# Both ends of a tile loop reordered, logits made in two halves: retention attention with a soft mixture of experts on one core

## The chip, the core and the metric

The kernel runs on one core of one Trainium2 chip. Its time is device microseconds of one execution. The kernel before took 230.43 us, the median of three runs (228.4 to 231.46).

## The reference

```
scores = q @ k.T / 8                      # q, k, v: 8 batches, 8 heads, 576 positions, 64 wide
x = ((scores * decay[head]) @ v)          # decay = gamma ** (i - j) for i >= j, else 0; no softmax
x = x as 4608 rows of 512                 # heads side by side
logits = x @ phi                          # 512 x 32: 8 experts of 4 slots
d = softmax of logits over the 4608 rows
slot_input = d.T @ x                      # 32 rows of 512
slot_out[e] = relu(slot_input[e] @ w1[e]) @ w2[e]     # 512 -> 1024 -> 512, for each expert
c = softmax of logits over the 32 slots
out = c @ slot_out                        # 4608 x 512
```

All of it is float32. Two steps look at every row before anything can follow: the softmax over rows and the sum that makes the slots' inputs.

## The kernel before, in words

The rows are worked off as 36 tiles of 128 rows. For each pair of batches there are nine tiles: four chunks of 128 positions for each of the two batches in turn (`z` is 0 or 1), and one tile with the last 64 positions of both (`z` is 2). A tile's input (k, transposed q and v, 512 columns each, 768 KB together) is loaded into one of four slots of the tile `qb`.

A tile `i` of the loop goes through these steps, in this order on TensorE (PE):

- `scores(i)` multiplies transposed k (`kts`) with q (L165); VectorE (DVE) multiplies the result with the mask `mt` into `sts`, in two halves (L169).
- `inter(i)` adds what earlier chunks contribute, from the running state `sbs` (L184; not in the first chunk of a batch).
- `k_transpose(i + 1)` turns the next tile's k (L156), and ScalarE (ACT) copies it to `kts` (L157); `scale(i + 1)` lets GpSimd (POOL) multiply v by a decay (L144, needs table `vt`) and, where a chunk begins, makes the table `xt` from `gt` and `cf` (L146, L149).
- a share of the softmax work of four tiles that are already done (below).
- `values(i)` multiplies `sts` with v (L192); DVE multiplies the result with `xt` and writes the tile's x, transposed, into a ring of eight (`rg`, L195).
- `state(i)` updates the running state (L204) and ACT copies it (L206).

Group g is tiles 4g to 4g+3. Its softmax work is spread over tiles 4g+4 to 4g+7: in the first, `comb_3` of the group before and the logits (L226) with the running maximum and, behind `state`, the exponential; in the second and third, the transposes of the four x (L212), of the exponentials (L253) and of the logits (L271); in the fourth `slot_sums` (L260), which adds the group to the running sum `acc` with a rescaling factor.

Each engine executes its instructions in the order of the program, as written; a wait holds up all that is behind it on that engine. Loads of tiles and of expert weights (64 units of 512 KB) are all issued by SyncE (SP); the tables are issued by ACT at the start. 38 units go to tiles of their own (`ws`): four at the start, then one per tile. Seven more go where the loop's own buffers come free (`qb`, `sts`). The last 19 units wait until an earlier unit has been used: `release` issues the next load into that unit's tile, or, once all 64 are issued, keeps the tile for outputs.

After the loop the last group is worked off, then `lrun` and `acc` give the slots' inputs (L380, L394, L397), and the experts' first products begin with four units (L437, the first release), then the second products (L458) and the outputs (L478 to L484), 18 stores of 512 KB.

Of the kernel before, what the change touches and what calls it, by code (L numbers as in the profile page):

```python
# [8 lines left out]
F32 = mybir.dt.float32  # L9
# [28 lines left out]
def retention_softmoe(ctx, tc, qkv, wts, phi, mtab, vtab, gtab, ctab, msel, out):  # L38
    nc = tc.nc
# [12 lines left out]
    ps_x, ps_st, ps_t = psum("ps_x", 2), psum("ps_st", 1), psum("ps_t", 3)  # L52
# [4 lines left out]
    qb = const("qb", NQ * 1536)  # L57
    ws = [const(f"ws{i}", 1024) for i in range(NW)]
# [21 lines left out]
    unit_tile = []  # L80

    def load_w(t):
        if len(unit_tile) < 64:
            nc.sync.dma_start(out=t, in_=wts[len(unit_tile)])
            unit_tile.append(t)
            return True
        return False

    def load_t(t, parts=((0, 1536),)):
        for lo, hi in parts:  # L90
            nc.sync.dma_start(out=qb[:, t % NQ * 1536 + lo:t % NQ * 1536 + hi], in_=qkv[t][:, lo:hi])

    load_t(0, ((0, 512), (512, 1024), (1024, 1536)))
    for x, y in ((vt, vtab), (mt, mtab), (cf, ctab), (gt, gtab)):
        nc.scalar.dma_start(out=x, in_=y)
    load_t(1)
    load_w(ws[0])
    load_t(2)
    load_w(ws[1])
    load_t(3)  # L100
    load_w(ws[2])
    load_w(ws[3])
    late = [(phs, phi), (ms, msel)]

    wz = ets
# [47 lines left out]
    def k_transpose(t):  # L153
        pt = ps_t.tile([P, 512], F32, name="pt")
        for a in range(NP):
            nc.tensor.transpose(pt[:, a * P:(a + 1) * P], part(t, 0)[:, a * P:(a + 1) * P], ident)  # L156
        nc.scalar.copy(out=kts, in_=pt)  # L157
# [17 lines left out]
    def inter(t):  # L175
        p, c, z = order[t]
        if c == 0:
            return
        x = X_of(t)
        for y in ((z,) if z < 2 else (0, 1)):  # L180
            cols = slice(0, P) if z < 2 else R[y]
            for a in range(NP):
                for j in range(2):
                    nc.tensor.matmul(x[R[a % 2], j, a // 2, cols], lhsT=sb[R[j], y, a, :], rhs=qT(t)[R[j], a, cols],  # L184
                                     start=(a < 2 and y == (0 if z == 2 else z)), stop=True, skip_group_check=True)
# [19 lines left out]
                                 start=(c == 0 and z == 0 and a == 0), stop=True, skip_group_check=True)  # L205
        nc.scalar.copy(out=sb[:, z], in_=pst[:, z])  # L206

    def x_transpose(t, pt=None, eng=None):
        if pt is None:
            pt = ps_t.tile([P, 512], F32, name="pt")  # L210
        for a in range(NP):
            nc.tensor.transpose(pt[:, a * P:(a + 1) * P], xT[t][:, a * P:(a + 1) * P], ident)  # L212
        if eng is nc.vector:
            nc.vector.tensor_copy(out=xT[t], in_=pt)  # L214
        else:
            nc.scalar.copy(out=xT[t], in_=pt)  # L216
# [3 lines left out]

    galpha = {}

    def logit_products(pl, g, tiles):
        for a in range(NP):
            for i in tiles:
                nc.tensor.matmul(pl[i * NS:(i + 1) * NS, :], lhsT=phs[:, a, :], rhs=xT[4 * g + i][:, a * P:(a + 1) * P],  # L226
                                 start=(a == 0), stop=(a == NP - 1), skip_group_check=True)

    def logits(g):
        pl = ps_t.tile([P, 512], F32, name="pt")[:, 0:P]  # L230
        logit_products(pl, g, range(4))
        nc.scalar.copy(out=lt[:, g, :], in_=pl)
        no, nn = nrun[(g + 1) % 2], nrun[g % 2]
        if g == 0:
            nc.vector.tensor_reduce(out=nn, in_=lt[:, g, :], axis=AX.X, op=ALU.max, negate=True)
        else:
            ng = sm("ng")
            nc.vector.tensor_reduce(out=ng, in_=lt[:, g, :], axis=AX.X, op=ALU.max, negate=True)
            nc.vector.tensor_tensor(out=nn, in0=ng, in1=no, op=ALU.min)
# [11 lines left out]
    def e_transpose(g):  # L251
        pe = ps_t.tile([P, 512], F32, name="pt")[:, 0:P]
        nc.tensor.transpose(pe, ets, ident)  # L253
        nc.scalar.copy(out=ens, in_=pe)

    def slot_sums(g, pp=None):
        if pp is None:
            pp = ps_t.tile([P, 512], F32, name="pt")
        for i in range(4):
            nc.tensor.matmul(pp[i * NS:(i + 1) * NS, :], lhsT=ens[:, i * NS:(i + 1) * NS], rhs=xT[4 * g + i],  # L260
                             start=True, stop=True, skip_group_check=True)
        if g == 0:
# [6 lines left out]
    def comb_1(g):  # L269
        pn = ps_t.tile([P, 512], F32, name="pt")[:, 0:P]  # L270
        nc.tensor.transpose(pn, lt[:, g, :], ident)  # L271
        ln = pn.rearrange("p (i s) -> p i s", i=4)
        cmx = sm("cmx", 4)
        nc.vector.tensor_reduce(out=cmx, in_=ln, axis=AX.X, op=ALU.max)
        cc = cn.rearrange("p (i s) -> p i s", i=4)
        nc.vector.tensor_tensor(out=cc, in0=ln, in1=cmx.unsqueeze(2).broadcast_to([P, 4, NS]), op=ALU.subtract)
        nc.scalar.activation(out=cn, in_=cn, func=AF.Exp, scale=1.0)
# [10 lines left out]
    def comb_3(g):  # L288
        pc = ps_t.tile([P, 512], F32, name="pt")[:, 0:P]
        nc.tensor.transpose(pc, cn, ident)  # L290
        nc.scalar.copy(out=lt[:, g, :], in_=pc)

    k_transpose(0)
    scale(0)
    for i in range(NT):
        g, r = divmod(i - 4, 4)
        scores(i)
        inter(i)
        if i + 1 < NT:
            k_transpose(i + 1)  # L300
            scale(i + 1)
        if g >= 0:
            if r == 0:
                if g:
                    comb_3(g - 1)
                logits(g)
            elif r == 1:
                x_transpose(4 * g)
                x_transpose(4 * g + 1)
                e_transpose(g)  # L310
            elif r == 2:
                x_transpose(4 * g + 2)
                x_transpose(4 * g + 3)
                comb_1(g)
            else:
                slot_sums(g)
        if i == NT - 1:
            pl = ps_st.tile([P, 512], F32, name="pst")[:, 0:P]
            logit_products(pl, NG - 1, range(3))
        values(i)  # L320
        state(i)
        if g >= 0:
            if r == 0:
                expo(g)
            if r == 2:
                comb_2(g)
        if i + NQ < NT:
            load_t(i + NQ)
        if late and i > 0:
            x, y = late.pop(0)  # L330
            nc.sync.dma_start(out=x, in_=y)
        if len(unit_tile) < NW:
            load_w(ws[len(unit_tile)])
    while len(unit_tile) < NW:
        load_w(ws[len(unit_tile)])
    for u in range(6):
        load_w(qb[:, u * 1024:(u + 1) * 1024])
    load_w(sts)

# [6 lines left out]
    g = NG - 1  # L346
    no, nn = nrun[(g + 1) % 2], nrun[g % 2]
    delta, far = ms[:, 0:P], ms[:, P:P + NS]
    x_transpose(4 * g)
    x_transpose(4 * g + 1, eng=nc.vector)  # L350
    logit_products(pl, g, range(3, 4))
    ng = sm("ng")
    nc.vector.tensor_reduce(out=ng, in_=pl, axis=AX.X, op=ALU.max, negate=True)
    nc.vector.tensor_tensor(out=nn, in0=ng, in1=no, op=ALU.min)
    rs = sm("rs")
    nc.scalar.activation(out=ets, in_=pl, func=AF.Exp, bias=nn, scale=1.0, accum_out=rs)
    x_transpose(4 * g + 2, eng=nc.vector)
    x_transpose(4 * g + 3, eng=nc.vector)
    pm = ps_x.tile([P, 2, 512], F32, name="sx")[:, 0, 0:P]
    nc.tensor.transpose(pm, nn.broadcast_to([P, P]), ident)  # L360
    e_transpose(g)
    alpha = sm("alpha")
# [10 lines left out]
    dl = sm("dl", NS)  # L373
    nc.vector.tensor_scalar(out=dl, in0=delta[:, 0:NS], scalar1=fa, scalar2=None, op0=ALU.mult)
    nc.vector.scalar_tensor_tensor(out=lrun, in0=lrun, scalar=alpha, in1=rs, op0=ALU.mult, op1=ALU.add)
    slot_sums(g)
    nc.scalar.copy(out=lt[:, g, :], in_=pl)
    comb_3(g - 1)
    pd = ps_t.tile([P, 512], F32, name="pt")
    nc.tensor.matmul(pd[:, 0:NS], lhsT=lrun.broadcast_to([P, P]), rhs=dl, start=True, stop=True)  # L380
    rv = sm("rv", NS)
# [197 lines left out]
```

## Time and profile before

| | |
|---|---|
| the profiled execution | 231.0 us |
| its span, first to last instruction | 229.2 us |
| PE busy, with 3994 matmuls and 3994 weight loads | 208.5 us (91%) |
| DVE, ACT, POOL busy | 115.0, 77.0, 61.2 us |
| moved by DMA | 72.59 MB, mean 317 GB/s |
| mean granted TensorE clock | 0.967 of full |

Busy shares are averages over three different stages: the start, the loop of tiles (to about 161 us) and the experts. A bracket at the end of a timeline's row holds the idle time of that engine just before it and what ended it; "issue" means that nothing which the profile shows was waited for. PE's times are modelled at their ends, so matmuls overlap slightly in the rows.

### The profile page before, as it was taken

What the parts mean: (1) busy time and instruction counts of PE and PEld (TensorE: products, weight loads), DVE (VectorE), ACT (ScalarE), POOL (GpSimd) and SP (SyncE); (2) the same over time, 40 slices, a digit from 0 to 9 for tenths busy, and PEclk for the clock granted to TensorE, in tenths of its full rate; (3) what the DMA queues carried; (4) which work ended last, traced back from release to release, by engine and by line L of the source; (5) the groups of instructions that cost most, each with busy time, mean ns of one, the idle gap of its engine ahead of it and who ended that gap; (6) DMA issues with size and microseconds to landing.
All of it is one profiled execution on the core that took longest, in us unless ns stands there. A gap on an engine that the chain in (4) does not pass through costs nothing.

```text
span 229.2 us, 8978 instructions
## 1 busy us (share of the span) xinstructions
PE 208.5 (91%) x3994; PEld 158.2 (69%) x3994; DVE 115.0 (50%) x234; ACT 77.0 (34%) x191; POOL 61.2 (27%) x65
## 2 busy tenths in 40 slices
PE   8498969999989999999999999999979999999910
PEld 7387859788779788789788789789752235555600
DVE  1245425847644866864764855755672201045820
ACT  2121244154235235255245154155130101136710
POOL 1461454242351335244144315341310000000000
PEclk9889999999999999999999999999997999999975
DMA  7999996789896789988778979898640999989996
GB/s 206 387 417 406 409 357 239 251 302 345 322 343 237 274 274 349 321 324 306 280 283 323 329 261 375 298 370 295 206 182 16 378 416 412 407 342 377 396 405 246
DMA packets 18181, 72.59 MB, mean 317 GB/s; under 512 B 2272, under 2 KB 2528, under 8 KB 18144
## 3 DMA queue, kind: packets, MB, share of 16 engines
q1 hardware_dynamic: 17568, 71.47, 84.1%
q8 instruction: 31, 0.51, 0.9%
q10 hardware_dynamic: 576, 0.56, 0.7%
q14 instruction: 6, 0.05, 0.1%
HBM read 62.58 MB, written 9.44 MB: 314 GB/s over the span
## 4 chain that ended last, share of the span: by engine, by line
PE 83%; DMA 7%; DVE 3%; issue 2%; SPq 1%; ACT 0%; DVEq 0%
PE sx L192 16%; PE sx L165 11%; PE pt L156 8%; DMA qb<-in_qkv 7%; PE po L437 7%; PE pt L212 7%; PE pt L458 6%; PE pst L204 6%; PE sx L184 5%; PE po L478 5%; PE pt L226 4%; PE pt L260 3%; PE pst L226 1%; PE pt L271 1%; DVE rg L214 1%
## 5 line engine op out<-in xcount | busy, mean ns | idle before, releaser
L144 POOL TENSOR_TENSOR qb<-qb,vt 128x512 f32<-128x512 f32 x36 | 37.6, 1045 | 86.1 <-DMA qb<-in_qkv 50.6
L169 DVE TENSOR_TENSOR sts<-sx,mt 128x512 f32<-128x512 f32 x72 | 46.3, 684 | 16.6 <-PE sx L165 16.6
L192 PE MATMUL sx<-sts,qb 128*64 128x128 f32 x576 | 40.5, 283 | 0.5 <-POOL xt L146 0.3
L195 DVE TENSOR_TENSOR rg<-sx,xt 128x512 f32<-128x512 f32 x36 | 24.9, 691 | 31.4 <-PE sx L192 31.0
L157 ACT COPY kts<-pt 128x512 f32<-128x512 f32 x36 | 21.1, 587 | 56.9 <-PE pt L156 55.1
L192 PEld LDWEIGHTS sx<-sts,qb 128*64 128x64 f32 x576 | 31.4, 139 | 11.4 <-issue 5.5
L165 PE MATMUL sx<-qb,kts 64*64 64x128 f32 (+1 forms) x1152 | 32.6, 250 | 0.7 <-ACT kts L157 0.7
L165 PEld LDWEIGHTS sx<-qb,kts 64*64 64x64 f32 x1152 | 27.2, 133 | 3.8 <-ACT kts L157 1.1
L156 PE MATMUL pt<-ident,qb 128*128 128x128 f32 x144 | 24.5, 294 | 3.2 <-DMA qb<-in_qkv 3.2
L206 ACT COPY sbs<-pst 128x256 f32<-128x256 f32 x32 | 11.9, 372 | 36.0 <-PE pst L204 36.0
L156 PEld LDWEIGHTS pt<-ident,qb 128*128 128x128 f32 x144 | 15.8, 145 | 8.3 <-issue 4.9
L184 PE MATMUL sx<-qb,sbs 64*64 64x128 f32 (+1 forms) x512 | 18.4, 257 | 2.8 <-issue 2.8
L204 PE MATMUL pst<-qb 128*64 128x64 f32 x512 | 20.5, 223 | 0.0
L204 PEld LDWEIGHTS pst<-qb 128*64 128x64 f32 x512 | 19.6, 139 | 0.0
L483 DVE COPY ws<-po 128x512 f32<-128x512 f32 x18 | 11.7, 687 | 15.6 <-PE po L478 15.4
L216 ACT COPY rg<-pt 128x512 f32<-128x512 f32 x33 | 17.9, 597 | 4.7 <-PE pt L212 4.7
L146 POOL TENSOR_TENSOR xt<-gt,cf 128x512 f32<-128x512 f32 x16 | 16.7, 1042 | 10.2 <-DVE rg L195 7.6
L212 PE MATMUL pt<-ident,rg 128*128 128x128 f32 x144 | 18.8, 273 | 0.0
L212 PEld LDWEIGHTS pt<-ident,rg 128*128 128x128 f32 x144 | 16.2, 140 | 0.4 <-issue 0.4
L437 PE MATMUL po<-ws,rg 128*32 128x512 f32 x128 | 16.0, 643 | 0.4 <-DVE rg L397 0.4
L184 PEld LDWEIGHTS sx<-qb,sbs 64*64 64x64 f32 x512 | 14.1, 134 | 3.2 <-issue 3.1
L478 PE MATMUL po<-kts,lt 32*128 32x256 f32 x144 | 12.4, 413 | 0.1
(87 smaller groups left out, 168.5 us busy)
## 6 DMA issues: line engine op xcount, KB each, us to landing
ws<-in_wts SPq DMA_DIRECT2D x57, 512.0 KB, 7.7
qb<-in_qkv SPq DMA_DIRECT2D x35, 768.0 KB, 6.3
out<-ws SPq DMA_DIRECT2D x18, 512.0 KB, 5.0
qb<-in_wts SPq DMA_DIRECT2D x6, 512.0 KB, 6.2
qb<-in_qkv SPq DMA_DIRECT2D x3, 256.0 KB, 3.6
sts<-in_wts SPq DMA_DIRECT2D x1, 512.0 KB, 5.1
mt<-in_mtab ACTq DMA_DIRECT2D x1, 256.0 KB, 4.0
gt<-in_gtab ACTq DMA_DIRECT2D x1, 256.0 KB, 7.7
```

Source lines behind the costliest of these rows:

```text
L144: nc.gpsimd.tensor_tensor(out=v, in0=v, in1=vt[:, c, :].unsqueeze(2).broadcast_to([P, H, D]), op=ALU.mult)
L156: nc.tensor.transpose(pt[:, a * P:(a + 1) * P], part(t, 0)[:, a * P:(a + 1) * P], ident)
L157: nc.scalar.copy(out=kts, in_=pt)
L165: nc.tensor.matmul(sp[R[z], j, a, lo:P], lhsT=kT[R[j], a, z * D:(z + 1) * D], rhs=qT(t)[R[j], a, lo:P], start=True, stop=True, skip_group_ ...
L169: nc.vector.tensor_tensor(out=sT[:, j].rearrange("p (s o) i -> p s o i", s=2), in0=sp[:, j].rearrange("p (s o) i -> p s o i", s=2), in1=m, ...
L184: nc.tensor.matmul(x[R[a % 2], j, a // 2, cols], lhsT=sb[R[j], y, a, :], rhs=qT(t)[R[j], a, cols], start=(a < 2 and y == (0 if z == 2 else ...
L192: nc.tensor.matmul(x[R[a % 2], j, a // 2, :], lhsT=vn(t)[:, 2 * a + j, :], rhs=sT[:, j, a, :], start=(c == 0 and a < 2), stop=True, skip_g ...
L195: nc.vector.tensor_tensor(out=xT[t].rearrange("p (j s i) -> p j s i", j=2, s=2), in0=x, in1=xtab(t).rearrange("p (j s) i -> p j s i", j=2) ...
L204: nc.tensor.matmul(pst[R[j], z, a, :], lhsT=kn(t)[:, 2 * a + j, :], rhs=vn(t)[:, 2 * a + j, :], start=(c == 0 and z == 0 and a == 0), stop ...
L212: nc.tensor.transpose(pt[:, a * P:(a + 1) * P], xT[t][:, a * P:(a + 1) * P], ident)
L437: nc.tensor.matmul(ph[nh][i * NS:(i + 1) * NS, :], lhsT=sims[:, kp, c, 4 * eh + i, :], rhs=w[:, c, :], start=(n % 4 == 0 and c == 0), stop ...
L478: nc.tensor.matmul(po[i // 2][:, i % 2, n * W:(n + 1) * W], lhsT=lt[r, g, :], rhs=so[r, lo:hi], start=True, stop=True, tile_position=(i * ...
```

## The change

At the start, the v part of tile 0 is issued by ACT, behind the table `vt` and ahead of `mt`, `cf` and `gt`; SP issues k and q of tile 0 and then tiles 1, 2 and 3. No weights are loaded before tile 2; from there it is one unit per tile, and two per tile in the last four tiles. In tile 0, `values(0)` now stands ahead of `k_transpose(1)`.

In the loop the logits of a group are made in two halves: `logits_1` takes two of the four 128-row pieces of the contraction in tile 4g+4, `logits_2` the other two in tile 4g+5. All later steps of the group move back by one tile; `slot_sums` stands in tile 4g+8. Group 7 is closed up at the end by one tile.

After the loop, all four tiles of the last group get their logits together, behind the first two transposes of x, whose copies go to `qb` in place of the ring. The load into the first part of `qb` is issued after the last `slot_sums`. Eight matmuls whose result nobody reads (`keep_warm`) are put between the steps that follow.

```diff
-    load_t(0, ((0, 512), (512, 1024), (1024, 1536)))
-    for x, y in ((vt, vtab), (mt, mtab), (cf, ctab), (gt, gtab)):
+    load_t(0, ((0, 512), (512, 1024)))
+    nc.scalar.dma_start(out=vt, in_=vtab)
+    nc.scalar.dma_start(out=qb[:, 1024:1536], in_=qkv[0][:, 1024:1536])
+    for x, y in ((mt, mtab), (cf, ctab), (gt, gtab)):
         nc.scalar.dma_start(out=x, in_=y)
     load_t(1)
-    load_w(ws[0])
     load_t(2)
-    load_w(ws[1])
     load_t(3)
-    load_w(ws[2])
-    load_w(ws[3])
...
+    def logits_1(g):
+        glogits[g] = ps_t.tile([P, 512], F32, name="pt")[:, 0:P]
+        logit_products(glogits[g], [xT[4 * g + i] for i in range(4)], range(4), (0, 1))
+
+    def logits_2(g):
+        pl = glogits.pop(g)
+        logit_products(pl, [xT[4 * g + i] for i in range(4)], range(4), (2, 3))
         nc.scalar.copy(out=lt[:, g, :], in_=pl)
...
+    for g in range(NG - 1):
+        i, last = 4 * g + 4, g == NG - 2
+        put(before, i, logits_1, g)
+        put(before, i if last else i + 1, logits_2, g)
+        put(behind, i if last else i + 1, expo, g)
+        k = i + 1 if last else i + 2
+        put(before, k, x_transpose, 4 * g)
+        put(before, k, x_transpose, 4 * g + 1)
+        put(before, k, e_transpose, g)
+        put(before, k + 1, x_transpose, 4 * g + 2)
+        put(before, k + 1, x_transpose, 4 * g + 3)
+        put(before, k + 1, comb_1, g)
+        put(behind, k + 1, comb_2, g)
+        put(before, k + 2, slot_sums, g)
+        if not last:
+            put(before, k + 3, comb_3, g)
...
         scores(i)
         inter(i)
+        if i == 0:
+            values(i)
         if i + 1 < NT:
             k_transpose(i + 1)
             scale(i + 1)
...
-        if i == NT - 1:
-            pl = ps_st.tile([P, 512], F32, name="pst")[:, 0:P]
-            logit_products(pl, NG - 1, range(3))
-        values(i)
+        for step in before.get(i, ()):
+            step()
+        if i:
+            values(i)
         state(i)
...
-        if len(unit_tile) < NW:
-            load_w(ws[len(unit_tile)])
+        for _ in range(0 if i < 2 else 1 if i + NQ < NT else 2):
+            if len(unit_tile) < NW:
+                load_w(ws[len(unit_tile)])
...
-    for u in range(6):
+    for u in range(1, 6):
         load_w(qb[:, u * 1024:(u + 1) * 1024])
...
-    x_transpose(4 * g)
-    x_transpose(4 * g + 1, eng=nc.vector)
-    logit_products(pl, g, range(3, 4))
+    xl = [xT[4 * g + i] for i in range(4)]
+    x_transpose(4 * g, out=qb[:, 0:512])
+    x_transpose(4 * g + 1, nc.vector, qb[:, 512:1024])
+    pl = ps_st.tile([P, 512], F32, name="pst")[:, 0:P]
+    logit_products(pl, xl, range(4))
...
+    def keep_warm(n):
+        for _ in range(n):
+            nc.tensor.matmul(pw, lhsT=ident, rhs=ident, start=True, stop=True)
...
+    keep_warm(2)
     slot_sums(g)
+    load_w(qb[:, 0:1024])
     nc.scalar.copy(out=lt[:, g, :], in_=pl)
     comb_3(g - 1)
+    keep_warm(4)
...
+    keep_warm(2)
```

The start, first on SP's queue, before and then in the change (`ws` are weights, `phs` is phi, `512` or `1536` are columns of a tile's input):

```order
L567 UNCONDITIONAL_BRANCH
L91 DMA qb<-in_qkv 128x512 x3
L91 DMA qb<-in_qkv 128x1536
L84 DMA ws_73<-in_wts 128x1024
L91 DMA qb<-in_qkv 128x1536
L84 DMA ws_74<-in_wts 128x1024
L91 DMA qb<-in_qkv 128x1536
L84 DMA ws_75<-in_wts 128x1024
L84 DMA ws_76<-in_wts 128x1024
L91 DMA qb<-in_qkv 128x1536
```

```order
L590 UNCONDITIONAL_BRANCH
L91 DMA qb<-in_qkv 128x512 x2
L91 DMA qb<-in_qkv 128x1536 x5
L342 DMA phs<-in_phi 128x128
L91 DMA qb<-in_qkv 128x1536
L342 DMA ms<-in_msel 128x192
L84 DMA ws_73<-in_wts 128x1024
L91 DMA qb<-in_qkv 128x1536
```

The four weight units that stood between the first tiles are gone from there; the first one now follows the load of tile 6. On PE in tile 0, from its last matmul of scores to the first of tile 1:

```order
L165 MATMUL sx<-qb,kts 64x128
L156 MATMUL pt<-ident,qb 128x128 x4
L192 MATMUL sx<-sts,qb 64x128 x8
L204 MATMUL pst<-qb 64x64 x8
L165 MATMUL sx<-qb,kts 64x128
```

```order
L163 MATMUL sx<-qb,kts 64x128
L190 MATMUL sx<-sts,qb 64x128 x8
L154 MATMUL pt<-ident,qb 128x128 x4
L202 MATMUL pst<-qb 64x64 x8
L163 MATMUL sx<-qb,kts 64x128
```

The eight matmuls of values and the four transposes of tile 1's k have changed places.

The end of the loop on PE: tile 35 from the last group's `slot_sums` on, where `rg_111` and `rg_112` hold the last four tiles' x and `pst` their logits:

```order
L260 MATMUL pt<-rg_114,ens 32x512 x2
L226 MATMUL pst<-rg_111,phs 32x128 x2
L226 MATMUL pst<-rg_112,phs 32x128
...
L192 MATMUL sx<-sts,qb 64x128 x8
L212 MATMUL pt<-ident,rg_111 128x128 x8
L226 MATMUL pst<-rg_112,phs 32x128 x4
L212 MATMUL pt<-ident,rg_112 128x128 x8
L360 MATMUL sx<-ident,nrun_132 128x128
```

```order
L265 MATMUL pt<-rg_114,ens 32x512 x2
L190 MATMUL sx<-sts,qb 64x128 x8
L209 MATMUL pt<-ident,rg_111 128x128 x8
L225 MATMUL pst<-rg_111,phs 32x128 x2
L225 MATMUL pst<-rg_112,phs 32x128 x2
...
L209 MATMUL pt<-ident,rg_112 128x128 x8
L379 MATMUL sx<-ident,nrun_132 128x128
```

The logits of three tiles ahead of values and of the fourth behind it have become one block of four tiles behind the first transposes.

The last place is on PE between that group's exponentials (`ets`) and the first expert (`po`):

```order
L253 MATMUL pt<-ident,ets 128x128
L260 MATMUL pt<-rg_111,ens 32x512 x2
L260 MATMUL pt<-rg_112,ens 32x512 x2
L290 MATMUL pt<-ident,cn 128x128
L380 MATMUL pt<-dl,lrun 128x32
L394 MATMUL pt<-dl,acc 128x32 x4
L437 MATMUL po<-ws_73,rg_113 32x512
```

```order
L258 MATMUL pt<-ident,ets 128x128
L377 MATMUL sx<-ident 128x128 x2
L265 MATMUL pt<-qb,ens 32x512 x2
L265 MATMUL pt<-rg_112,ens 32x512 x2
L295 MATMUL pt<-ident,cn 128x128
L377 MATMUL sx<-ident 128x128 x4
L402 MATMUL pt<-dl,lrun 128x32
L416 MATMUL pt<-dl,acc 128x32 x4
L377 MATMUL sx<-ident 128x128 x2
L460 MATMUL po<-ws_73,rg_113 32x512
```

The eight extra matmuls stand in three places, and two of the four x are read from `qb`, so that `rg_111` has its last reader earlier, in the logits.

## Rows read from the trace of the kernel before

**Rows 1.** The page, busy time, share of the span and instructions of each engine.

```profile
PE 208.5 (91%) x3994; PEld 158.2 (69%) x3994; DVE 115.0 (50%) x234; ACT 77.0 (34%) x191; POOL 61.2 (27%) x65
```

**Rows 2.** Timeline, tile 4 and the end: start us, us, engine, line, work [idle before].

```profile
26.14 1.08 PE L226 MATMUL pt<-rg,phs 128*32 128x128 f32 x32
...
161.67 1.28 DVE L169 TENSOR_TENSOR sts<-sx,mt 128x512 f32<-128x512 f32 x2
162.65 1.39 PE L226 MATMUL pst<-rg,phs 128*32 128x128 f32 x24
163.97 1.09 PE L192 MATMUL sx<-sts,qb 128*64 128x128 f32 x16
166.02 1.06 PE L226 MATMUL pst<-rg,phs 128*32 128x128 f32 x8
168.89 1.20 PE L260 MATMUL pt<-rg,ens 128*32 128x512 f32 x8 [0.35 <-ACT ens L254]
170.00 1.05 DVE L374 TENSOR_SCALAR dl<-ms,fa 128x32 f32<-128x32 f32 x1 [0.36 <-ACT fa L372]
170.06 0.95 POOL L402 MEMSET rg<- 128x1024 f32 x1 [5.27 <-PE pt L260]
172.85 3.20 PE L437 MATMUL po<-ws,rg 128*32 128x512 f32 x16 [0.37 <-DVE rg L397]
...
180.37 5.36 PE L437 MATMUL po<-ws,rg 128*32 128x512 f32 x48
```

**Rows 3.** Windows of the end: us, busy per engine, PEclk, DMA share, GB/s.

```profile
174.00:175.00 1.00, 1.00 (x12) 0.21 (x4) 0.00 (x0) 0.00 (x0) 0.00 (x0) 0.50 0.00 0
...
224.00:226.00 2.00, 0.00 (x0) 0.00 (x0) 0.00 (x0) 0.00 (x0) 0.00 (x0) 0.50 1.01 401
```

**Rows 4.** Timeline of SP's queue: the loads that wait for a release.

```profile
176.05 18.27 SPq L84 DMA_DIRECT2D ws<-in_wts  x19
```

**Rows 5.** Timeline of the start.

```profile
1.17 0.46 ACTq L95 DMA_DIRECT2D mt<-in_mtab  x1
2.14 0.46 ACTq L95 DMA_DIRECT2D gt<-in_gtab  x1
7.33 1.29 DVE L169 TENSOR_TENSOR sts<-sx,mt 128x512 f32<-128x512 f32 x2 [5.28 <-PE sx L165]
9.71 1.12 PE L156 MATMUL pt<-ident,qb 128*128 128x128 f32 x4 [2.45 <-DMA qb<-in_qkv]
9.98 1.04 POOL L146 TENSOR_TENSOR xt<-gt,cf 128x512 f32<-128x512 f32 x1 [2.62 <-DMA gt<-in_gtab]
10.76 1.98 PE L192 MATMUL sx<-sts,qb 128*64 128x128 f32 x16
15.07 1.16 PE L192 MATMUL sx<-sts,qb 128*64 128x128 f32 x16 [0.32 <-POOL xt L146]
```

**Rows 6.** The page, DMA issues: KB each, us from issue to landing.

```profile
mt<-in_mtab ACTq DMA_DIRECT2D x1, 256.0 KB, 4.0
gt<-in_gtab ACTq DMA_DIRECT2D x1, 256.0 KB, 7.7
```

**Rows 7.** The page, groups of instructions: busy us, mean ns, idle before.

```profile
L195 DVE TENSOR_TENSOR rg<-sx,xt 128x512 f32<-128x512 f32 x36 | 24.9, 691 | 31.4 <-PE sx L192 31.0
```

**Rows 8.** Timeline of the early loop: PE's waits.

```profile
22.11 0.63 PE L156 MATMUL pt<-ident,qb 128*128 128x128 f32 x4 [0.78 <-DMA qb<-in_qkv]
...
31.49 0.66 PE L184 MATMUL sx<-qb,sbs 64*64 64x128 f32 x15 [1.86 <-issue]
...
66.63 0.66 PE L184 MATMUL sx<-qb,sbs 64*64 64x128 f32 x13 [0.93 <-issue]
```

**Rows 9.** The page, DMA queues: packets, MB, share of 16 engines.

```profile
q8 instruction: 31, 0.51, 0.9%
```

**Rows 10.** Windows of the start and the early loop.

```profile
10.00:12.00 2.00, 2.00 (x16) 1.67 (x16) 0.00 (x0) 0.59 (x1) 2.00 (x2) 0.50 1.02 425
...
30.00:32.00 2.00, 0.51 (x15) 0.42 (x14) 0.89 (x2) 0.00 (x0) 0.79 (x1) 1.00 1.04 384
```

More of the change, by code (lines that the diff above doesn't have):

```diff
@@ L206, in state, with x_transpose @@
         nc.scalar.copy(out=sb[:, z], in_=pst[:, z])
-    def x_transpose(t, pt=None, eng=None):
-        if pt is None:
-            pt = ps_t.tile([P, 512], F32, name="pt")
+    def x_transpose(t, eng=nc.scalar, out=None):
+        pt = ps_t.tile([P, 512], F32, name="pt")
         for a in range(NP):
             nc.tensor.transpose(pt[:, a * P:(a + 1) * P], xT[t][:, a * P:(a + 1) * P], ident)
+        if out is not None:
+            xT[t] = out
         if eng is nc.vector:
@@ L221, in retention_softmoe, with logit_products @@
     galpha = {}
-    def logit_products(pl, g, tiles):
-        for a in range(NP):
+    def logit_products(pl, xs, tiles, steps=range(NP)):
+        for a in steps:
             for i in tiles:
-                nc.tensor.matmul(pl[i * NS:(i + 1) * NS, :], lhsT=phs[:, a, :], rhs=xT[4 * g + i][:, a * P:(a + 1) * P],
+                nc.tensor.matmul(pl[i * NS:(i + 1) * NS, :], lhsT=phs[:, a, :], rhs=xs[i][:, a * P:(a + 1) * P],
                                  start=(a == 0), stop=(a == NP - 1), skip_group_check=True)
-    def logits(g):
-        pl = ps_t.tile([P, 512], F32, name="pt")[:, 0:P]
-        logit_products(pl, g, range(4))
+    glogits = {}
+    def logits_1(g):
[4 more added lines that the diff above has]
+        logit_products(pl, [xT[4 * g + i] for i in range(4)], range(4), (2, 3))
         nc.scalar.copy(out=lt[:, g, :], in_=pl)
@@ L291, in comb_3, with put @@
         nc.scalar.copy(out=lt[:, g, :], in_=pc)
+    before, behind = {}, {}
+    def put(where, i, f, *a):
+        where.setdefault(i, []).append(lambda: f(*a))
+    for g in range(NG - 1):
[14 more added lines that the diff above has]
+            put(before, k + 3, comb_3, g)
     k_transpose(0)
@@ L295, in retention_softmoe @@
     for i in range(NT):
-        g, r = divmod(i - 4, 4)
         scores(i)
         inter(i)
+        if i == 0:
+            values(i)
         if i + 1 < NT:
@@ L301, in retention_softmoe @@
             scale(i + 1)
[L302 to L307, printed above, removed]
-                x_transpose(4 * g)
[L309 to L316, printed above, removed]
-        if i == NT - 1:
-            pl = ps_st.tile([P, 512], F32, name="pst")[:, 0:P]
-            logit_products(pl, NG - 1, range(3))
-        values(i)
-        state(i)
[L322 to L326, printed above, removed]
+        for step in before.get(i, ()):
+            step()
+        if i:
+            values(i)
+        state(i)
+        for step in behind.get(i, ()):
+            step()
         if i + NQ < NT:
@@ L348, in retention_softmoe @@
     delta, far = ms[:, 0:P], ms[:, P:P + NS]
-    x_transpose(4 * g)
-    x_transpose(4 * g + 1, eng=nc.vector)
-    logit_products(pl, g, range(3, 4))
+    xl = [xT[4 * g + i] for i in range(4)]
[3 more added lines that the diff above has]
+    logit_products(pl, xl, range(4))
     ng = sm("ng")
@@ L356, in retention_softmoe @@
     nc.scalar.activation(out=ets, in_=pl, func=AF.Exp, bias=nn, scale=1.0, accum_out=rs)
-    x_transpose(4 * g + 2, eng=nc.vector)
-    x_transpose(4 * g + 3, eng=nc.vector)
-    pm = ps_x.tile([P, 2, 512], F32, name="sx")[:, 0, 0:P]
+    x_transpose(4 * g + 2, nc.vector)
+    x_transpose(4 * g + 3, nc.vector)
+    pm, pw = (ps_x.tile([P, 2, 512], F32, name="sx")[:, 0, 0:P] for _ in range(2))
+    def keep_warm(n):
+        for _ in range(n):
+            nc.tensor.matmul(pw, lhsT=ident, rhs=ident, start=True, stop=True)
     nc.tensor.transpose(pm, nn.broadcast_to([P, P]), ident)
```

## The prediction, on record before the changed kernel ran

> **What bounds the kernel now.** I read the page first, then the timeline from both ends, then windows of the places where PE stands still. The page has PE busy for 208.5 of 229.2 us [rows 1], so what can be won is time in which PE waits, runs at its lower clock, or does a piece of work twice. In the timeline the loop's stretch between 67 and 160 us shows no wait of PE over 0.15 us, so no reordering there can give much. The losses stand in three places, and the reader is to see them in these rows.
>
> At the start PE waits 2.45 us for tile 1 and then, with the granted clock at 0.50 (the 1.2 GHz level), takes 1.98 us for values that take 1.16 at full clock [rows 5, 10]. In the early loop it waits 0.78 us for tile 4, and twice for nothing that the profile shows, 1.86 and 0.93 us [rows 8]. At the end the logits of the last group are made in two pieces, 1.39 and 1.06 us, and the first experts run at 0.50 of the clock: 16 matmul instructions in 3.20 us, where later 48 take 5.36, so 1.79 for 16 [rows 2, 3].
>
> Behind that the end hangs on DMA as much as on PE. The queue moves nothing at 174 us [rows 3]; the loads that wait for the first experts begin at 176.05 [rows 4]; 19 units and 18 stores, 37 times 524,288 bytes or 19.4 MB, take 48 us at the 401 GB/s of the last window [rows 3], and 176 + 48 is 224, where that window still moves data. So what brings the first experts' end forward brings the end of the kernel forward by the same time, and PE's part of the end moves with it.
>
> **The change part by part.**
>
> *Start.* Without the four weight units, 2 MB or 5 us at 401 GB/s, tile 4 comes in time: 0.78 us gone [rows 8]. Against that stands the order on ACT's queue. The mask table was issued at 1.17 and landed 4.0 us later, at 5.2; `gt` was issued at 2.14 and landed at 9.8, and POOL took it up at 9.98 [rows 5, 6]. The two stand 4.7 us apart, because `gt` shares the engines with a tile. Now v takes the mask's place, and the mask comes at 5.2 to 9.8 (I take 8.5, nearer to `gt`, since a tile is beside it too), and `gt` 4.7 us behind the mask's place at the latest, so 9.8 to 14.5; I take 12.9. The masks of tile 0 then start at 8.5 for 7.33, which still lets values go at about 9.2 for 10.76. But `gt` holds POOL's 1.04 us for `xt` [rows 5], this DVE's 0.69 us on tile 0's x [rows 7], and that, on a queue in order, the masks of tile 1, whose first half takes 0.65: 12.9 + 1.04 + 0.69 + 0.65 and 0.1 for hand-overs is 15.4, where values of tile 1 began at 15.07. That is +0.3, with bounds of -0.3 (never late) and +2.0 (`gt` at 14.5). The lower clock in this stretch stays, because PE still waits for about 2 us. Start: -0.5.
>
> *The wait of 1.86 us.* It falls in the middle of one block of matmuls, while DMA is at 1.04 of its capacity [rows 8, 10]. Queue q8 brings 31 pieces of instructions [rows 9]; PE has 3994 matmuls and as many weight loads [rows 1], 258 per piece. I read the wait as PE's own program coming late behind data. With no weights before tile 2 there is less data; I take 1.5 of 1.86 off, with bounds of 0 and 1.86. The Trainium skill, Runtime: NRT & Kernel Launch, section Instruction fetch mechanics, has PE's program come in blocks of 256 instructions, which the trace agrees with, and calls the cost of a block's boundary mostly hidden. By that rule the wait would not be code and nothing would be won here; the sum would be 1.5 us higher. The wait of 0.93 us at 66.63 [rows 8] lies where loads are as before: 0.
>
> *Logits in halves, steps moved by a tile.* 32 instructions for four tiles take 1.08 us [rows 2], so a half takes 0.54, and nothing is added. Slot sums at about 1.06 and half the logits now share one tile, the other half and one transpose the next: PE's extra work per tile is less even than it was, about 1.6, 0.8, 1.0 and 1.0 us. It costs nothing as long as each tile has enough between scores and values to hide DVE's 1.28 us of masks [rows 2]; the lightest still has transposes of k (0.63, [rows 8]) and 0.8, and the contribution of earlier chunks (0.66) in all but eight tiles. Price 0, bounds -0.3 and +0.5.
>
> *Two units per tile in the last four tiles.* SP has no tile left to load there and nothing to wait for, so 8 units, 4.2 MB or 10 us, go out together. More waits as that of 1.86 us can come of it: 0 to 1.86, I take +0.3.
>
> *Logits of the last group in one block.* One pass for four tiles instead of 1.39 and 1.06 us. Values of tile 35 began at 163.97, behind the 1.39; the masks end at 161.67 + 1.28 = 162.95 [rows 2], and these are late next: values at 163.05. -0.9.
>
> *GpSimd's clearing of `rg`.* It was held by the last slot sums and ran at 170.06; in the change it is held by the logits and runs right behind them, beside DVE's running minimum. At 170.00 DVE's small multiplication took 1.05 us and ended at 171.05, with POOL's memset, 171.01 [rows 2]. If the minimum is held in the same way, exponentials and all that follows come later, by up to 0.9; I take +0.45. The Trainium skill, SBUF — State Buffer, in its list on the shared port pair, lets a DVE instruction with two inputs from SBUF block only against a GpSimd operation that reads SBUF, and a memset reads none. By that rule this term would be 0 and the sum 0.45 us lower.
>
> *Extra matmuls.* The nearest row to one 128x128 matmul of two instructions is the four transposes at full clock, 0.63 us, 0.16 per instruction [rows 8]; at the lower level it was 0.28 [rows 5]. So eight cost 2.5 us of PE by that, 4.5 at the other end, and less if they pipeline. Most fall into idle time: 0.35 us ahead of slot sums, 0.37 ahead of the first expert [rows 2], and the wait for `dl`, which came at 171.05. I take +0.45; bounds 0 and +1.2.
>
> *The clock.* If PE is kept from falling to 0.50, the first 16 instructions take 1.79 for 3.20 us and the next small ones gain a little: -1.45. The release of the first units moves by -1.4. Bounds 0 and -1.5.
>
> *The load of `qb` behind the last slot sums* goes into a stretch in which DMA is idle [rows 3], and its unit is used last of the 45: 0.
>
> **The sum.** -0.5 - 1.5 + 0.3 - 0.9 + 0.45 + 0.45 - 1.45 = -3.15 us. The profiled execution took 231.0 us (span 229.2), 0.6 above the median of the runs; against the median, 230.43 - 3.15 = 227.3 us.
>
> **The rivals.**
>
> 1. *The clock falls all the same.* The extra matmuls stand between narrow ones (32 columns) and waits, and the fall came after just such a stretch [rows 3]. Then the last term is 0: 228.7. For it: the start fell after a wait of 2.45 us. Against it: the wait of 1.86 us lowered nothing. Chance 0.13.
> 2. *The start gives nothing back.* `gt` lands near 14.5 and PE's unnamed waits have nothing to do with loads, as the rule on code would have it: -3.15 + 1.7 + 1.5 = 0, so about 230; with one of the two, 228.7 to 229. Chance 0.17, most of it on one of the two: 229.
> 3. *Slower.* The burst of weights at tiles 32 to 35 starves PE of its program. Place: the tiles behind 147 us; price 1.86 each [rows 8]. Two such waits, 3.7 us less the 0.3 already in the sum, take the whole gain; three make 227.3 - 0.3 + 5.6 = 232.6. For it: DMA was full when the wait of 1.86 us came. Against it: it was full for most of the first 30 us, and one long wait came of it. Chance 0.07.
> 4. *More waits go than I count.* Both unnamed waits vanish (-0.36 more, and -0.93), the burst costs nothing (-0.3), and the memset holds nothing (-0.45): 225.3. Against it: nothing in the change thins the loads around 66 us. Chance 0.22.
>
> The forecast itself has 0.41.
>
> **How the numbers follow.** Predicted 227.3. The range goes from 224.8 (rival 4 with another 0.5) to 230.2 (rival 2 whole); it leaves out rival 3 and the tails. A change of under 2%, here 4.6 us, is about what a measurement of this kernel cannot tell from none. Faster by more needs under 225.8: most of rival 4, 0.17, and 0.11 of the forecast's spread: 0.28. Slower by more needs over 235: 0.04. The rest, 0.68, lies within.
>
> **What would show it.** Start: POOL's first `xt` near 13 us, values of tile 1 at about 15.4, no wait of PE on tile 4. Early loop: PE's "issue" idle in tiles 4 to 7 under 0.5 us. Loop: tiles as long as before. End: values of tile 35 right behind slot sums; the minimum taking 0.4 us or more beside a POOL memset; the granted clock at 1.00 through the first experts, which take 1.8 us; releases beginning some 1.4 us sooner after them. The prediction is wrong if the clock falls again, if PE shows new waits behind tile 31, or if the loop's tiles change their length.

## The result, and the profile after

The changed kernel took 227.05 us, the median of 15 runs (224.47 to 229.06), against 230.43 before (15 runs, 227.92 to 234.1); the ratio is 0.986, with a 95% interval of 0.982 to 0.991. The ratios in this text come from the faster runs of each kernel alone, so they are not quite the quotients of the medians. The profiled execution took 228.06 us, 1.0 over its median, with a span of 226.28 us against 229.22. Runs of one kernel differ by 1% or more either way, so the timelines below place the parts and the ratios weigh them.

The timeline of the changed kernel's start, as in [rows 5]. Line numbers have moved by about two: L167 is the mask, L190 values, L144 `xt`, L163 scores, L154 the transposes of k.

```profile
8.93 1.29 DVE L167 TENSOR_TENSOR sts<-sx,mt 128x512 f32<-128x512 f32 x2 [6.89 <-DMA mt<-in_mtab]
9.72 1.98 PE L190 MATMUL sx<-sts,qb 128*64 128x128 f32 x16 [2.46 <-issue]
12.38 1.04 POOL L144 TENSOR_TENSOR xt<-gt,cf 128x512 f32<-128x512 f32 x1 [6.06 <-DMA gt<-in_gtab]
13.73 1.56 PE L163 MATMUL sx<-qb,kts 64*64 64x128 f32 x32
16.19 1.16 PE L190 MATMUL sx<-sts,qb 128*64 128x128 f32 x16
...
24.47 0.90 PE L163 MATMUL sx<-qb,kts 64*64 64x128 f32 x32
```

The mask table now ends the masks' wait at 8.93 for 7.33, `gt` lets `xt` begin at 12.38 for 9.98, and scores of tile 1 run at the lower clock (1.56 us; 0.90 later): the granted clock is 0.50 from 9.0 to 15.8 us, where before it was 0.50 from 9.5 to 12.9. Values of tile 1 begin 1.1 us later than before. Nothing waits for tile 4 any more, and its scores begin at 24.47, where they began at 24.15: in these two executions the start lost 0.3 us. Before, the scores of tiles 4 and 35 stood here:

```profile
24.15 0.99 PE L165 MATMUL sx<-qb,kts 64*64 64x128 f32 x31
...
160.48 0.90 PE L165 MATMUL sx<-qb,kts 64*64 64x128 f32 x32
```

In the early loop, for [rows 8], one larger unnamed wait is left, and a new one comes in tile 35 (the transposes behind its values are counted to it here):

```profile
37.48 0.27 PE L190 MATMUL sx<-sts,qb 128*64 128x128 f32 x1 [0.86 <-issue]
...
163.86 0.70 PE L209 MATMUL pt<-ident,rg 128*128 128x128 f32 x5 [0.59 <-issue]
```

The end, for [rows 2] (L225 is the logits, L367 and L368 the running minimum, L425 the memset, L393 `dl`, L377 the extra matmuls, L460 the first experts):

```profile
159.41 0.90 PE L163 MATMUL sx<-qb,kts 64*64 64x128 f32 x32
161.70 1.09 PE L190 MATMUL sx<-sts,qb 128*64 128x128 f32 x16
164.50 1.08 PE L225 MATMUL pst<-rg,phs 128*32 128x128 f32 x32
165.63 0.95 POOL L425 MEMSET rg<- 128x1024 f32 x1 [1.91 <-PE pst L225]
165.67 0.29 DVE L367 TENSOR_REDUCE ng<-pst 128x1 f32<-128x128 f32 x1 [0.37 <-PE pst L225]
165.99 0.16 DVE L368 TENSOR_TENSOR nrun<-ng,nrun 128x1 f32<-128x1 f32 x1
168.49 0.24 DVE L393 TENSOR_SCALAR dl<-ms,fa 128x32 f32<-128x32 f32 x1 [0.36 <-ACT fa L391]
168.69 1.06 PE L377 MATMUL sx<-ident 128*128 128x128 f32 x8
171.36 1.92 PE L460 MATMUL po<-ws,rg 128*32 128x512 f32 x16
173.30 7.11 SPq L84 DMA_DIRECT2D ws<-in_wts  x11
```

The windows there (the third number from the end is the clock), for [rows 3]:

```profile
172.00:173.00 1.00, 1.00 (x13) 0.13 (x4) 0.00 (x0) 0.00 (x0) 0.00 (x0) 1.00 0.00 0
...
222.00:224.00 2.00, 0.00 (x0) 0.00 (x0) 0.00 (x0) 0.00 (x0) 0.00 (x0) 0.50 0.95 375
```

Values of tile 35 begin 2.29 us behind its scores, where before it was 3.49 (163.97 in [rows 2]). The logits are one pass of 1.08 us. The minimum takes 0.16 us beside the memset, and `dl`, no longer beside it, 0.24 for 1.05. The first 16 expert instructions run at full clock in 1.92 us for 3.20, and the first release comes at 173.30 for 176.05 [rows 4]: 2.75 us sooner. The kernel's span ends 2.94 us sooner. So the end did follow the release, as the prediction had it.

### The profile page after: what moved, and what is told of

The parts are those of the page before. It is cut to its first block, busy times and chain, and to the rows that moved or that the text cites. A ratio compares the mean times of both kernels' runs of the same rounds, so it can differ in the third digit from the quotient of the medians.

```text
span 226.3 us, 9015 instructions
## 1 busy us (share of the span) xinstructions
PE 208.8 (92%) x4010; PEld 159.7 (71%) x4010; DVE 115.9 (51%) x234; ACT 76.5 (34%) x191; POOL 61.1 (27%) x65
## 4 chain that ended last, share of the span: by engine, by line
PE 90%; issue 3%; ACT 2%; DVE 1%; ACTq 0%
PE sx L190 16%; PE sx L163 13%; PE pt L154 10%; PE pst L202 7%; PE pt L481 6%; PE po L460 6%; PE pt L209 6%; PE sx L182 6%; PE po L501 5%; PE pt L265 4%; PE pt L225 3%; PE pt L108 2%; ACT kts L155 1%; PE pt L276 1%; PE sx L377 1%
## 5 line engine op out<-in xcount | busy, mean ns | idle before, releaser
L167 DVE TENSOR_TENSOR sts<-sx,mt 128x512 f32<-128x512 f32 x72 | 46.3, 684 | 18.7 <-PE sx L163 11.6
L190 PE MATMUL sx<-sts,qb 128*64 128x128 f32 x576 | 40.8, 283 | 3.4 <-issue 3.3
L193 DVE TENSOR_TENSOR rg<-sx,xt 128x512 f32<-128x512 f32 x36 | 24.9, 691 | 29.4 <-PE sx L190 24.3
L190 PEld LDWEIGHTS sx<-sts,qb 128*64 128x64 f32 x576 | 31.6, 139 | 10.2 <-issue 7.1
L163 PE MATMUL sx<-qb,kts 64*64 64x64 f32 (+1 forms) x1152 | 33.1, 254 | 0.7 <-ACT kts L155 0.7
L163 PEld LDWEIGHTS sx<-qb,kts 64*64 64x64 f32 x1152 | 27.8, 136 | 3.8 <-ACT kts L155 1.1
L154 PE MATMUL pt<-ident,qb 128*128 128x128 f32 x144 | 25.0, 297 | 0.1
L202 PE MATMUL pst<-qb 128*64 128x64 f32 x512 | 21.2, 225 | 0.2 <-issue 0.2
L144 POOL TENSOR_TENSOR xt<-gt,cf 128x512 f32<-128x512 f32 x16 | 16.6, 1040 | 14.4 <-DVE rg L193 8.4
L154 PEld LDWEIGHTS pt<-ident,qb 128*128 128x128 f32 x144 | 16.1, 147 | 5.6 <-issue 4.8
L182 PE MATMUL sx<-qb,sbs 64*64 64x128 f32 (+1 forms) x512 | 17.5, 257 | 0.1
L215 ACT COPY rg<-pt 128x512 f32<-128x512 f32 x32 | 17.4, 598 | 0.1
L460 PE MATMUL po<-ws,rg 128*32 128x512 f32 x128 | 14.6, 595 | 0.1
L501 PE MATMUL po<-kts,lt 32*128 32x256 f32 x144 | 12.4, 413 | 0.1
```

The costliest lines, as they stand in the source:

```text
L163: nc.tensor.matmul(sp[R[z], j, a, lo:P], lhsT=kT[R[j], a, z * D:(z + 1) * D], rhs=qT(t)[R[j], a, lo:P], start=True, stop=True, skip_group_ ...
L167: nc.vector.tensor_tensor(out=sT[:, j].rearrange("p (s o) i -> p s o i", s=2), in0=sp[:, j].rearrange("p (s o) i -> p s o i", s=2), in1=m, ...
L190: nc.tensor.matmul(x[R[a % 2], j, a // 2, :], lhsT=vn(t)[:, 2 * a + j, :], rhs=sT[:, j, a, :], start=(c == 0 and a < 2), stop=True, skip_g ...
L193: nc.vector.tensor_tensor(out=xT[t].rearrange("p (j s i) -> p j s i", j=2, s=2), in0=x, in1=xtab(t).rearrange("p (j s) i -> p j s i", j=2) ...
L202: nc.tensor.matmul(pst[R[j], z, a, :], lhsT=kn(t)[:, 2 * a + j, :], rhs=vn(t)[:, 2 * a + j, :], start=(c == 0 and z == 0 and a == 0), stop ...
L460: nc.tensor.matmul(ph[nh][i * NS:(i + 1) * NS, :], lhsT=sims[:, kp, c, 4 * eh + i, :], rhs=w[:, c, :], start=(n % 4 == 0 and c == 0), stop ...
```

## The experiments

The first repeats the changed kernel; the next three undo one part of the change each, on the same chip. The later ones ran on two other chips; each ratio is against the kernel before, run beside it. In this section "waits" are TensorE's unnamed waits of over 0.1 us that end at a piece of its program (shown in the next section), and the stretch from scores of tile 35 to the first expert is called the close; it is given without the wait in it.

**The changed kernel again.**

> The changed kernel once more, as the measure for the three beside it. Theory: the gain is made at the end of the loop (one block of logits, about 1.2 us, and TensorE's clock kept at 1.00 through the first experts, about 1.3 us) and by fewer unnamed waits of TensorE (1.0 us here against 2.9 us before); the start gives nothing. Expected 227, ratio 0.985 to 0.99. Rival: the even spread of the softmax work shortens the tiles. Both expect the same of this run.

Measured: 0.988 [0.983, 0.993]. Its profile has scores of tile 4 at 24.42, no wait before 98 us, then 0.50 and 1.58, and 1.13 in tile 35; the first execution had 0.14, 0.86, 0.18 and 0.59. The waits move from run to run. Close: 11.4 us.

**The old start.**

```diff
-    load_t(0, ((0, 512), (512, 1024)))
-    nc.scalar.dma_start(out=vt, in_=vtab)
-    nc.scalar.dma_start(out=qb[:, 1024:1536], in_=qkv[0][:, 1024:1536])
+    load_t(0, ((0, 512), (512, 1024), (1024, 1536)))
...
+    load_w(ws[0])    # and ws[1] to ws[3] behind tiles 2 and 3
...
-        for _ in range(0 if i < 2 else 1 if i + NQ < NT else 2):
+        for _ in range(1):
```

> The changed kernel with the start of the kernel before: v of tile 0 on the SP queue, weights between the first tiles, values of tile 0 behind the transposes of tile 1, one weight unit per tile from tile 0. Theory: tile 4's scores begin at 24.1 to 24.2 us, no later than the 24.47 of the changed kernel, and the early weights bring back an unnamed wait of TensorE of 1 us or more in tiles 4 to 7; total 0 to +1 us against the changed kernel. Rival (the new start is what wins): 2 us or more slower, with tile 4 later than 25 us.

Measured: 0.983 [0.980, 0.987], scores of tile 4 at 23.18, waits of 0.86 and 1.37 at 24 and 30 us, 0.43 later, none in tile 35. It is not slower than the changed kernel; the rival falls, and the theory's cost of up to 1 us does not show either. The edit takes the two units per tile at the end back as well, and with them went the wait in tile 35.

**The old places of the softmax steps.**

```diff
-        put(before, i, logits_1, g)
-        put(before, i if last else i + 1, logits_2, g)
+        put(before, i, logits, g)      # both halves; all later steps one tile earlier
```

> The changed kernel with the softmax steps at the places of the kernel before (all four logit pieces in one tile, slot sums one tile earlier); start and end as changed. Theory: nothing, within 0.5 us of the changed kernel, and tiles 8 to 35 as long as there within what unnamed waits differ by. Rival (the spread shortens the tiles): 1.4 us slower, the difference seen between scores of tile 4 and of tile 35.

Measured: 0.996 [0.987, 1.004], above the changed kernel's 0.988 with overlapping intervals, while the median lies 0.3 us under the one beside it (227.94 and 228.24): the totals decide nothing. From scores of tile 4 to those of tile 35 it is 135.5 us with 1.65 of waits; the changed kernel has 134.9 with 1.2 and 135.7 with 2.1. Without the waits that is 133.9, 133.8 and 133.6: the spread does nothing to the tiles, and the rival's 1.4 us are not there.

**The old logits of the last group.**

```diff
+        if i == NT - 1:
+            logit_products(pl, [xT[NT - 4 + j] for j in range(3)], range(3))
...
-    x_transpose(4 * g, out=qb[:, 0:512])
-    x_transpose(4 * g + 1, nc.vector, qb[:, 512:1024])
-    logit_products(pl, xl, range(4))
+    x_transpose(4 * g)
+    x_transpose(4 * g + 1, nc.vector)
+    logit_products(pl, {3: xT[4 * g + 3]}, (3,))
```

> The changed kernel with the last group's logits as before: three tiles ahead of values of tile 35, the fourth behind the first transposes; the eight extra matmuls stay. Theory: 1.0 to 1.3 us slower than the changed kernel, from scores of tile 35 to the first expert 13.4 us in place of 12.0. Rival (the pass over three tiles was hidden behind the masks anyway): no difference, 12.0 us.

Measured: 0.992 [0.989, 0.995]; the close is 12.7 us (13.70 with a wait of 1.03) against 11.4 (11.95 with 0.59). The block is worth 1.3 us of the close; the totals do not tell the two kernels apart. This edit also puts POOL's memset back beside `dl`, which takes 1.08 us in it, so the 1.3 us hold both.

**No extra matmuls, in two executions.**

```diff
-        for _ in range(n):
+        for _ in range(0):
```

> The changed kernel without the eight extra matmuls. Theory: TensorE's clock falls to 0.50 during the first experts as in the kernel before; their first 16 matmul instructions take about 3.2 us for 1.92, the first release comes about 1.3 us later behind the first expert, and the total is 1 to 1.5 us longer. The first expert itself begins no earlier than with the extra matmuls, within 0.3 us. Rival (the clock stays up because the last group is worked off faster): the same time or up to 0.4 us less.

Measured: 0.9935 [0.989, 0.998]. But in its profile the clock stayed at 1.00 and the 16 instructions took 1.92 us; the close was 11.1 us, 0.3 shorter than with the extra matmuls. Theory missed in what it said of the clock, as far as this execution goes. The ratio lies above the changed kernel's two (0.986 and 0.988), as the theory had it, but the intervals overlap.

> A second look at the changed kernel without the extra matmuls. If the tighter end keeps the clock up by itself: 1.00 and 1.92 us again for the first 16 expert instructions. If the first look was chance: 3.2 us at 0.50.

In the second execution the clock fell. Its first experts and a window of them:

```profile
166.93 2.83 PE L460 MATMUL po<-ws,rg 128*32 128x512 f32 x16 [0.37 <-DVE rg L420]
```

```profile
168.00:169.00 1.00, 1.00 (x12) 0.03 (x3) 0.00 (x0) 0.00 (x0) 0.00 (x0) 0.50 0.00 0
```

**The old end as a whole, and the extra matmuls alone.** The first is the kernel with old logits, without the extra matmuls; the second adds the extra matmuls, at their places, to the kernel before.

> The changed kernel's start and loop with the end of the kernel before as a whole: logits of the last group in two pieces, copies in place, no extra matmuls, and so POOL's memset beside dl again. Theory now (without the extra matmuls the clock is kept up by the tighter end: dl takes 0.24 us in place of 1.05 and TensorE's wait ahead of the sums shrinks from 0.85 to 0.16): the clock falls to 0.50 again, the first 16 expert instructions take about 3.2 us, and from scores of tile 35 to the first release it is 15.5 us, against 13.6 to 13.9 with the new end. Rival (whether the clock falls depends on when the end comes, not on how it is built): the clock stays up, 1.92 us and about 14.2 us.

Measured: 1.000 [0.995, 1.004]. The clock fell and the 16 instructions took 2.62 us, less than the 3.2 expected. From scores of tile 35 to the first release it is 16.9 us, 15.0 without a wait of 1.85. `dl` is held by the memset again, as in [rows 2]:

```profile
170.30 1.05 DVE L394 TENSOR_SCALAR dl<-ms,fa 128x32 f32<-128x32 f32 x1 [0.36 <-ACT fa L392]
170.36 0.95 POOL L425 MEMSET rg<- 128x1024 f32 x1 [7.18 <-PE pt L265]
```

So new start and new loop with the old end gain nothing measurable.

> The kernel before with the eight extra matmuls alone. Theory now (either the tighter end or the extra matmuls is enough): clock at 1.00 in the first experts, 16 instructions in 1.92 us, first expert 0.2 to 0.5 us later behind scores of tile 35 than the 12.37 us before, total 1 us shorter. Rival (narrow matmuls and waits still let it fall): 3.2 us, total 0.3 us longer.

Measured: 0.992 [0.986, 0.998], clock at 1.00, 1.92 us; the close 12.3 us, no longer than the 12.4 before, since there the matmuls fit into the wait for `dl`. In the nine profiles with the extra matmuls the 16 instructions took 1.92 us each time; in five without them the clock fell in three (before, this old end, and the second of the two executions above). They keep the clock where otherwise it differs from execution to execution: it fell in both executions with the old end and without them, and in one of three with the new end.

**No weights during the loop.**

```diff
-        for _ in range(0 if i < 2 else 1 if i + NQ < NT else 2):
+        for _ in range(0):
```

> The changed kernel with no weights loaded during the loop: all 38 units are loaded behind it, so its end is far longer and only the loop is to be read. Theory (unnamed waits of TensorE are its program coming late behind data): no such wait over 0.2 us from tile 4 to tile 35, where the changed kernel's two traces have 1.5 to 3.5 us; scores of tile 35 at 158 us or earlier. Rival (code loading is hidden, and the waits have another cause): as many waits as with the weights, 1 us or more in sum.

With 186 GB/s from 30 to 140 us in place of 312, waits up to tile 34 fall to one of 0.46, in tile 26; scores of tile 35 begin at 158.11. One of 0.59 stands in tile 35, while SP issues the 38 units, one behind the other, from 143.96 on. The theory asked for none over 0.2, the rival for 1 us or more in sum. Each is half right in size, and other kernels with the weights had as little (next section), so this run alone does not show that loads make the waits. Their place decides what they are.

```profile
119.63 0.55 PE L154 MATMUL pt<-ident,qb 128*128 128x128 f32 x3 [0.46 <-issue]
...
162.56 0.71 PE L209 MATMUL pt<-ident,rg 128*128 128x128 f32 x5 [0.59 <-issue]
```

**v back on SP's queue**, all else as changed:

```diff
-    load_t(0, ((0, 512), (512, 1024)))
-    nc.scalar.dma_start(out=vt, in_=vtab)
-    nc.scalar.dma_start(out=qb[:, 1024:1536], in_=qkv[0][:, 1024:1536])
-    for x, y in ((mt, mtab), (cf, ctab), (gt, gtab)):
+    load_t(0, ((0, 512), (512, 1024), (1024, 1536)))
+    for x, y in ((vt, vtab), (mt, mtab), (cf, ctab), (gt, gtab)):
```

> The changed kernel with v of tile 0 on the SP queue as in the kernel before, so that the mask table and gt land as early as there; all else as changed. Theory (the tables pushed back by v are what the start loses): masks of tile 0 begin at 7.3 us for 8.93, xt at about 10 for 12.38, values of tile 1 near 13 for 16.19, scores of tile 4 at 21 to 22.5 for 24.4; total 2 us or more shorter than the changed kernel, 224 to 225.5. Rival (tile 1's landing near 9.7 us is the bound whatever the tables do): scores of tile 4 at 24, total unchanged.

Measured: 0.983 [0.977, 0.989]; `xt` at 9.71, values of tile 1 at 14.95, scores of tile 4 at 23.23. In this execution scores of tile 0 and values took 1.56 and 1.98 us, as at the lower clock (its record of the clock begins only at 13.6 us), so the start shows less than was expected. Scores of tile 0 at 1.56 us stand at the head of three executions with v on ACT's queue, too, and there scores of tile 4 begin at 23.71 to 23.89; here it is 23.23 and in the next kernel 23.48. Here, and then with the old softmax places:

```profile
6.36 1.56 PE L161 MATMUL sx<-qb,kts 64*64 64x128 f32 x32 [0.67 <-ACT kts L153]
...
23.23 0.90 PE L161 MATMUL sx<-qb,kts 64*64 64x128 f32 x32
```

```profile
6.36 1.56 PE L163 MATMUL sx<-qb,kts 64*64 64x128 f32 x32 [0.68 <-ACT kts L155]
...
23.80 0.90 PE L163 MATMUL sx<-qb,kts 64*64 64x128 f32 x32
```

Like with like, v's place is worth 0.2 to 0.7 us. In four further executions with v on ACT's queue, the changed kernel's two among them, the clock fell only behind the scores of tile 0 and rose later; they have 24.3 to 24.8 and are no measure for this one. The median, 224.62 us, lies in the 224 to 225.5 that the theory asked for, and 3.0 us under that of the changed kernel without extra matmuls beside it (227.65), though the ratio is not told apart from the changed kernel's. What made the rest of these 3 us stays open.

**The last weights issued by ACT**, in addition:

```diff
-                load_w(ws[len(unit_tile)])
+                load_w(ws[len(unit_tile)], nc.sync if i + NQ < NT else nc.scalar)
```

> As the kernel with v on the SP queue, and the weights of the last four tiles issued by ACT behind each tile's state in place of SP all at once. Theory: the unnamed waits of 0.5 to 1.1 us in tile 35 and the small ones in tiles 33 and 34 go, 0.5 to 1 us less than without. Rival (those waits come from all loads alike): no difference.

Measured: 0.978 [0.971, 0.985], not told apart from the one before. The wait in tile 35 is 0.39 here and 1.02 in the next kernel, so it did not go: four of the eight units still go out together there, as tile 35 has nothing that ACT waits for.

**The same without the extra matmuls.**

> v of tile 0 on the SP queue, weights of the last four tiles issued by ACT, no extra matmuls: the changed kernel without the parts that cost. Theory: 0.3 to 0.4 us less than with the extra matmuls, ratio to the kernel before 0.975 to 0.98. Rival (the extra matmuls are needed in some executions): 1 us more in those, ratio 0.98 to 0.985.

Measured: 223.28 us, 0.971 [0.966, 0.976], a little under the 0.975 to 0.98 that the theory asked for, and the fastest; its interval lies below the changed kernel's two (0.982 to 0.991 and 0.983 to 0.993). Its start:

```profile
7.33 1.29 DVE L165 TENSOR_TENSOR sts<-sx,mt 128x512 f32<-128x512 f32 x2 [5.28 <-PE sx L161]
8.12 1.21 PE L188 MATMUL sx<-sts,qb 128*64 128x128 f32 x16 [0.86 <-issue]
10.00 1.04 POOL L142 TENSOR_TENSOR xt<-gt,cf 128x512 f32<-128x512 f32 x1 [2.91 <-DMA gt<-in_gtab]
12.51 1.17 PE L188 MATMUL sx<-sts,qb 128*64 128x128 f32 x16 [0.33 <-DVE sts L165]
...
20.78 0.90 PE L161 MATMUL sx<-qb,kts 64*64 64x128 f32 x32
```

Masks and `xt` are as early as in [rows 5], PE waits 0.86 us in place of 2.46, and scores of tile 4 begin at 20.78, 3.7 us sooner than in the changed kernel. Most of that is the clock in the start, which v's place alone does not decide: here it was up (values 1.21 us for 1.98), as it was in the second execution without extra matmuls, where v is on ACT's queue and scores of tile 4 begin at 21.48. What raises it in some executions stays open, and so does whether PE's shorter wait helped to keep it up here; one execution cannot show it. That the extra matmuls can be left out is not shown either: the clock did not fall here, but it did in one of the two executions above.

## Why the prediction was right

The sum, -3.15 us, came out as -2.94 on the spans and -3.4 on the medians, but its terms did not all hold. That it came so near is in part luck: the start came out 0.8 us worse than its term, and the last group's logits (0.4) and the memset (0.45) better by as much. Three of the prediction's own signs went against it: the minimum was not held, 1.0 us of unnamed waits stood in tiles 4 to 7 for the 0.5 it allowed, and a new wait came behind tile 31, which it had named as a sign of being wrong.

*Start: -0.5 forecast, +0.3 measured.* The times of the tables were near (8.93 for 8.5, 12.38 for 12.9), values of tile 0 at 9.72 for 9.2. What failed is the step from there, values of tile 1 at 16.19 for 15.4: I let scores of tile 1 run at full clock, and DVE's masks of tile 1, held by `xt` and tile 0's x until 14.15, then waited for those scores until 15.35.

*The wait of 1.86 us: -1.5 forecast.* At its place the changed kernel waits 0.14 us, and 0.86 at the next. The reading as code is borne out. Counted from 0 along all of PE's instructions in order of their start (matmuls, weight loads and some 93 semaphore and drain instructions), the first instruction behind the waits of 1.86 and 0.93 before is number 961 and 2497, behind the four of the changed kernel 961, 1217, 5825 and 6849: each is 256 n + 193. In all twelve experiments' profiles, every unnamed wait of 0.4 us or more between 20 us and the end of tile 35 for which no DVE row stands in the bracket ends there as well, and 1.2 to 1.6 us behind the end of a piece on queue q8. So PE waits for its program. That fewer loads shorten these waits is less sure: between tiles 4 and 34 the three profiles with weights between the first tiles (before, old start, extra matmuls alone) have 2.7 to 3.0 us of it, the ten with weights from tile 2 on have 0 to 2.1, and 1.0 on average, and the one without weights in the loop has 0.46. The Trainium skill calls the cost of a block's boundary mostly hidden (Runtime: NRT & Kernel Launch, Instruction fetch mechanics). The trace agrees for most: of some 25 such places behind 20 us, one to four in each run show a wait. Those few cost 0.4 to 3.2 us in all, so here the cost is not nothing.

*Two units per tile at the end: +0.3 forecast, +0.6 here*, and 0.4 to 1.9 us in the ten profiles with two units per tile there, 0.9 on average, in tile 35; in the three without it none. Together the two terms gave about -0.9 on average for -1.2.

*Logits in halves: 0, as forecast.* *One block of logits: -0.9 forecast, -1.3 measured*: values of tile 35 did not wait for both halves of the masks (161.70, where the second half ended at 161.88), which is 1.2 us of it, and `dl` is no longer held.

*The memset: +0.45 forecast, 0 measured.* The minimum took 0.16 us beside it. That is what the Trainium skill says (SBUF — State Buffer, the list on the shared port pair), and the trace agrees: two SBUF inputs are not held by a memset. The 1.05 us of `dl`, one input and a scalar, had misled me, and its going was a gain that I did not count: 2.11 us from the slot sums to the products with `dl` for 2.31, with four extra matmuls in between, and 1.56 without them.

*Extra matmuls: +0.45 forecast, +0.3 measured. Clock: -1.45 forecast, -1.3 measured* where it fell before. Rival 1, that it falls all the same, was refuted in nine profiles; but the fall is not certain without them either, and where it came elsewhere the 16 instructions took 2.62 and 2.83 us, so on average the term is smaller than in my sum.

*Rival 2* was half right: the start gave nothing back, though `gt` landed near 12.3 us and not near 14.5. *Rival 3*, the burst, had the right mechanism with a lower price: one wait, not three. *Rival 4* was partly seen: the wait at 66 us is gone, by chance, since such waits come elsewhere in other runs.

## What to carry to other kernels

A wait that the profile puts down to nothing may be the engine's own program: count instructions, and see whether the waits sit at one place in 256. Fewer loads in flight there may shorten them (2.7 to 3.0 us here with weights between the first tiles, 1.0 on average without), but did not end them. Where tables are issued on a second queue, a large transfer put ahead of them delays every table behind it (here the mask table landed 7.2 us after its issue for 4.0, `gt` 9.6 for 7.7); ask which first operation needs which table. And before a change's sum is believed term by term, undo the terms one at a time: here the end (the close and the clock behind it) gave nearly everything, the spread nothing, and the start hid a loss that one transfer's place made, 0.2 to 0.7 us of it seen like with like. An execution's start depends on its clock more than on the order, so executions of the same kind of start are to be compared.

## What the runs showed of the hardware

At the first experts TensorE's clock fell in three of five executions without the extra matmuls, and in none of nine with eight plain 128x128 matmuls between the narrow ones; these cost 0.3 us. In the start it was up in some executions and down in others of nearly the same work, which moved the scores of tile 4 by 2 to 3 us. Where PE waited for a piece of its program, it went on 1.2 to 1.6 us after the piece's transfer ended, also with DMA at 186 GB/s. One SBUF input with a scalar took 1.05 to 1.08 us beside a POOL memset in four profiles and 0.24 in the ten in which the memset had run before; in those ten, two SBUF inputs took 0.16 us beside it.
